# Sums over keys with both partial sums on TensorE, and new orders for the first and the middle head pairs

## The chip, the cores and the metric

The kernel runs on one core of one Trainium2 chip. The metric is the device time of one execution, in microseconds (us), as the median of several runs; beside it stands one execution that the hardware profiler took, from which all rows come. TensorE is PE in the rows (PEld is its weight load), VectorE is DVE, ScalarE is ACT, GpSimd is POOL and SyncE is SP.

## What is computed

Attention over 4 x 8 heads with queries averaged in twos, then a soft mixture of 8 experts, then a gated layer. Cut to what matters:

```python
# attention: q, k, v are (4, 8, 1152, 64), here worked on as 16 pairs of heads
q_pool = q.reshape(B, H, S // 2, 2, D).mean(axis=3)
scores = scale * np.matmul(q_pool, k.transpose(0, 1, 3, 2))
scores = scores - np.max(scores, axis=-1, keepdims=True)
attn = np.exp(scores)
attn = attn / (np.sum(attn, axis=-1, keepdims=True) + 1e-09)   # the sums over keys
x = np.matmul(attn, v)                       # -> (2304, 512)
# soft mixture: logits = x @ phi, a softmax over tokens and one over slots,
# 32 slots through the experts' w1, relu, w2, and back to the tokens
# gated layer: rms norm, silu(xn @ w_gate) * (xn @ w_val) @ w_out
```

## The kernel before

**Stages.** First the attention, one pair of heads at a time (16 pairs, numbered 0 to 15 by `p`), with the mixture's logits worked in between; then the 8 experts; then the gated layer. While the pairs run, the 36 tiles of the gated layer's weights come in as 64-bit values, are converted to 32 bits (`load_64`, `abs_64`, `turn_64`) and are written away to DRAM (`spill`), to be read back at the end (`load`, kind "r").

**One pair.** A pair has 9 tiles of keys (`kt`) and 2 halves of queries (`h`), so 18 score steps. `qk` (step `q<kt><h>`) makes a score tile with 8 matmul records in PSUM and ACT takes its exponential `e` (L380). `add_e` (step `e<kt><h>`) adds the exponentials on POOL (L396) into two partial sums for each half, `acc[p, h, 0]` and `acc[p, h, 1]`: the first 5 or 6 tiles go into one, the others into the second (`PART`). `av` (step `v<kt>`) multiplies with the values into one PSUM tile that stays open over all 9 tiles. In the next pair `sum_up` (L413) joins the two partial sums: for pairs 0 to 13 by a transfer from SBUF to SBUF that POOL issues and that adds while it writes (L415), for pair 14 by DVE. Then `sums` (L419) sums over keys with a matmul against ones; it takes one partial sum, or both where the second one still exists (`n = 1 + ((p, hs[0], 1) in acc)`), as it does for pair 15.

**Beside it in each pair.** `m`, `ta` and `tb` are products for the next pair's row maxima (`wide_item`, each reduced by DVE, L322 to L335); `max_red`, `max_row` and `send_row` turn the maxima into a row and send it by four small transfers on SP's queue (L353, L354). `load_q`, `load_k`, `sum_q`, `high_q`, `low_q`, `round_k`, `less_k` and `rest_k` prepare the pair after next; `sum_q` and `rest_k` are accumulating transfers issued by POOL. `take_x` copies the finished values (xu), `inverse`, `recips` (the copy rr, L444) and `x_divide` divide them by the sums; `logit_add` adds to the logits. Every fourth pair has extra steps: `d_turn` and `d_exp` in pairs 4, 8 and 12, `d_back`, `d_copy` (the copy dn, L539), `slot_part` and `slot_turn` in pairs 5, 9 and 13, `c_turn` (ct, L585 and L587) in pairs 6, 10 and 14.

**What sets the order.** Each engine, and each queue of transfers, works in the order in which the program issues. That order is written out by hand in four lists of steps: `FIRST` for pair 0, `PLAN` for pairs 1 to 13, `LAST_2` for pair 14 and `LAST` for pair 15 (`order_of`). A step named three times is done in three parts: the three `abs_64` of a pair each convert the oldest raw weight that was loaded, the three `turn_64` each finish the oldest conversion on DVE, and the three `load_64` each load one. A step that has nothing to do is passed over.

**Room.** SBUF tiles come from pools of fixed numbers: `B` has 32 (exponentials, partial sums, rounded q), `A` 11, `C` 27. In PSUM the attention has four tiles (two banks each) for everything, one of which the values hold. A new tile waits until the last reader of the tile that it replaces is done. `keep_b` holds back a number of B tiles from the loads of weights.

Of the kernel before, what the change touches and what calls it, by code (L numbers as in the profile page):

```python
# [14 lines left out]
ALU = mybir.AluOpType  # L15
# [3 lines left out]
NP = 16  # L19
# [12 lines left out]
NMAX = 9  # L32
AHEAD = 0
FIRST = """
q00 e00 q10 round_k1 e10 q20 e20 m v00 m m v10 m v20 q30 round_k1 e30 q40 low_q e40 q50 e50 m v30 block_q1 m m v40 m
v50 row_0 q60 e60 q70 low_k e70 q80 e80 m v60 m m load_q v70 v80 q01 e01 q11 low_k e11 q21 e21 m v01 m load_k m v11
sum_q v21 q31 high_q e31 q41 e41 q51 e51 m v31 m load_v max_red v41 v51 max_row send_row q61 round_k e61 q71 e71 q81
e81 round_k less_k v61 v71 v81 block_q
"""
PLAN = """  # L40
load_q c_exp take_x m q00 rest_k sum_q sum_up q01 q10 sum_up m q11 q20 e00 e10 e20 load_k m q21 e01 m q30 e11 q31 q40
load_ew e21 m load_ew e31 q41 e41 e30 q50 q51 e40 m q60 q61 m e50 q70 e60 q71 m e51 q80 q81 e61 e71 m tb ta spill e70
v0 v1 high_q round_k abs_64 max_red sums turn_64 max_row x_logits inverse e80 send_row inverse load_64 v2 e81 turn_64
round_k pair_up logit_add v3 v4 block_q v5 load_64 v6 less_k d_back abs_64 low_q d_turn c_soft abs_64 turn_64 recips
x_turn d_copy slot_part c_turn slot_copy c_soft c_soft x_divide c_soft v7 load_64 x_divide drop_x d_exp v8 slot_turn
load_v
"""
LAST_2 = """
load_q c_exp take_x m q00 rest_k sum_q sum_up q01 load q10 sum_up m q11 load q20 e00 e10 e20 load_k m load q21 e01 m
load q30 e11 q31 load q40 load_ew e21 m load_ew e31 load q41 e41 e30 load q50 q51 e40 m load q60 load q61 m e50 q70  # L50
e60 q71 m e51 load q80 q81 e61 e71 m tb ta spill e70 v0 v1 high_q round_k abs_64 max_red sums turn_64 max_row x_logits
inverse e80 send_row inverse load_64 v2 e81 turn_64 round_k pair_up logit_add v3 v4 block_q v5 load_64 v6 less_k
d_back abs_64 low_q d_turn c_soft abs_64 turn_64 recips x_turn d_copy slot_part c_turn slot_copy c_soft c_soft
x_divide c_soft v7 load_64 x_divide drop_x d_exp v8 slot_turn load_v
"""
LAST = """
take_x q00 load_64 sum_up sum_up load_q load_k load q01 e00 e01 c_exp turn_64 load_ew load q10 load q11 spill e10 e11
# [39 lines left out]
def attention_softmoe_gated_kernel(ctx: ExitStack, tc: tile.TileContext, kT, qT, vv, ip, cst, w1, w2, wg, wv, wo, rg, out):  # L97
    nc = tc.nc
    dv, ac, pe, gp, sy = nc.vector, nc.scalar, nc.tensor, nc.gpsimd, nc.sync
# [11 lines left out]
    free = dict(size)  # L111
# [12 lines left out]
    def rel(tag, n=1):  # L124
        free[tag] += n
        assert free[tag] <= size[tag], tag
# [16 lines left out]
    def two(name, keep_a):  # L143

        if not pairs:
            tag = next((x for x in "WA" if free[x] > (keep_a if x == "A" else 0)), None)
            if not tag:
                return None
            us, t = carve(tag, F32, name)
            for i in range(0, len(us) - 1, 2):  # L150
                pairs.append((t[:, 512 * i:512 * i + 1024], us[i][1]))
            if len(us) % 2:
                singles.append(us[-1])
        return pairs.pop(0)

    keep_b = [99]

    def room(keep_a=0):
        return (len(singles) + 2 * len(pairs) + free["C"] + max(0, free["B"] - keep_b[0])
                + 3 * free["W"] + 2 * max(0, free["A"] - keep_a))  # L160

    def unit(name):

        if singles:
            return singles.pop(0)
        for tag in "CB":
            if free[tag] > (keep_b[0] if tag == "B" else 0):
                return take(tag, [128, 512], F32, name), lambda: rel(tag)
        t, drop = two(name, 0)
        singles.append((t[:, 512:1024], drop))  # L170
        return t[:, 0:512], drop
# [47 lines left out]
    tb = one.tile([128, 128], F32R, name="tb")  # L219
# [4 lines left out]
    mx3, xu, acc, avt, rr, lg, srow = ({} for _ in range(7))  # L224
# [186 lines left out]
        ac.copy(xu[p].rearrange("p (h q) -> p h q", h=2), avt.pop(p)[:, :, 0:HQ])  # L411

    def sum_up(p, h):  # L413
        if p < NP - 2:
            gp.dma_start(out=acc[p, h, 0], in_=acc.pop((p, h, 1)), accum_op=ALU.add)  # L415
        else:
            dv.tensor_tensor(out=acc[p, h, 0], in0=acc[p, h, 0], in1=acc.pop((p, h, 1)), op=ALU.add)
        rel("B")

    def sums(p, hs=(0, 1)):  # L420
# [229 lines left out]
    def load(n, keep_a=0, keep_c=0):  # L650

        for _ in range(n):
            if not stream:
                return
            kind, e, i = stream[-1]
            if kind == "r":
                if not free["C"]:
                    return
                w32[e, i] = unit("w32")
                sy.dma_start(out=w32[e, i][0], in_=away[e, i])  # L660
            else:
                if kind == "w1":
                    src = w1[e, 64 * i:64 * i + 128, :]
                else:
                    src = w2[e, 128 * i:128 * i + 256, :].rearrange("(c p) d -> p c d", p=128)
                if room(keep_a) < len(fresh) + 2 + keep_c:
                    return
                t = two(kind, keep_a)
                if t:
                    t, drop = t  # L670
                    sy.dma_start(out=t if kind == "w1" else t.rearrange("p (c d) -> p c d", c=2), in_=src)
                    x = [(t[:, 0:512], drop), (t[:, 512:1024], drop)]
                elif len(singles) + free["C"] + max(0, free["B"] - keep_b[0]) >= 2:
                    x = [unit(kind), unit(kind)]
                    for c in range(2):
                        sy.dma_start(out=x[c][0], in_=src[:, 512 * c:512 * c + 512] if kind == "w1" else src[:, c])
                else:
                    return
                for c in range(2):
                    ew[kind, e, i + c] = x[c]  # L680
            stream.pop()
# [23 lines left out]
    def side(p):  # L705
# [66 lines left out]
        if 0 < p < NP - 2:  # L772
            at("load_64", lambda i: load_64() if i < 2 or p % 2 or p < 11 else None)
            at("load_ew", lambda i: load(1, 99, KEEP_C + min(len(doubles), 4 * HELD + HELD_O)) if p >= FIRST_EW else None)
# [4 lines left out]
        if p == NP - 2:  # L779
            spill()  # L780
            assert not doubles
            at("load", lambda i: (keep_b.__setitem__(0, KEEP[3]), load(1, KEEP_A[0])))
        if p == NP - 1:
            at("load", lambda i: (spill(), keep_b.__setitem__(0, KEEP[0]), load(1, KEEP_A[1])))
        return sides

    with tc.manual_schedule():
# [127 lines left out]
        for h in range(2):  # L915
# [16 lines left out]
                         in1=al[:, :, None].to_broadcast([32, 3, 32]), op=ALU.mult)  # L932
# [375 lines left out]
```

## Time and profile before

| | us |
|---|---|
| median of 3 runs | 722.84 (721.96 to 726.03) |
| the profiled execution | 728.97 |
| its span, first to last instruction | 727.2 |
| PE busy | 677.9 (93%) |
| POOL busy | 479.2 (66%) |
| DVE busy | 434.0 (60%) |
| ACT busy | 402.6 (55%) |

A busy time is the sum of an engine's work, whatever it waited in between; the ends of matmuls are modelled, so a busy PE is not PE at its peak. Where an engine waits, the profile names the event that came last. The granted clock is TensorE's, 1.00 for 2.4 GHz; the lower of the two levels is 1.2 GHz.

### The profile page before, as it was taken

Reading aid. Unit: us, or ns where it says so; the run is one execution under the profiler, and the core shown is the slowest. Engines: PE = TensorE matmul, PEld = TensorE weight load, DVE = VectorE, ACT = ScalarE, POOL = GpSimd, SP = SyncE. Lnnn points to the kernel's source line nnn. Section 1 sums busy time; section 2 is a strip of 40 time slices with the busy share of each in tenths; the row PEclk is TensorE's granted clock in tenths of the full one; section 3 lists DMA queues with packets and bytes.
Section 4 is the critical chain, followed back from the end, with each engine's and each line's share of the span. In section 5 each row is a group of like instructions: output and inputs, shape, how many; then the busy total and the mean of one; then the engine's idle time right before and its main releaser. Section 6 shows DMA issues by size and latency. Waiting matters only on the chain.

```text
span 727.2 us, 17618 instructions
## 1 busy us (share of the span) xinstructions
PE 677.9 (93%) x7199; PEld 482.8 (66%) x7199; DVE 434.0 (60%) x597; ACT 402.6 (55%) x812; POOL 479.2 (66%) x393
## 2 busy tenths in 40 slices
PE   4999989999798999798999989999989999999998
PEld 2566766756467567475775766654467788888887
DVE  5756877767476777566878856632154755544420
ACT  2466866766467677565776753533155755444320
POOL 5589899889595997966899977401046955535320
PEclk9999999999899999999999999999999999999999
DMA  5144775975939569566495586899991000000000
GB/s 177 52 129 116 200 240 130 277 230 124 320 92 292 202 153 285 154 149 190 108 286 173 109 259 226 291 313 376 386 383 38 35 26 30 29 30 30 15 36 37
DMA packets 61793, 122.33 MB, mean 168 GB/s; under 512 B 6808, under 2 KB 20624, under 8 KB 61712
## 3 DMA queue, kind: packets, MB, share of 16 engines
q1 hardware_dynamic: 53792, 100.86, 39.5%
q0 software_dynamic: 7920, 20.35, 15.0%
q8 instruction: 56, 0.92, 0.5%
q14 instruction: 25, 0.20, 0.1%
HBM read 98.70 MB, written 14.16 MB: 155 GB/s over the span
## 4 chain that ended last, share of the span: by engine, by line
PE 65%; DMA 17%; ACT 6%; DVE 4%; SPq 4%; issue 3%; POOL 1%; ACTq 0%; POOLq 0%; DVEq 0%
PE yo L1209 19%; PE sc L378 18%; PE av L403 8%; DMA acc<-acc 5%; PE mxp L321 3%; DMA raw<-in_wo_dram 3%; DMA qs<-in_qT_dram 3%; PE gv L1161 3%; DMA raw<-in_wg_dram 2%; PE hin L974 2%; PE so L999 2%; SPq L354 2%; DMA w<-away 1%; DMA raw<-in_wv_dram 1%; PE pp L549 1%
## 5 line engine op out<-in xcount | busy, mean ns | idle before, releaser
L396 POOL TENSOR_TENSOR acc<-acc,e 128x576 f32<-128x576 f32 x153 | 230.8, 1517 | 15.4 <-ACT e L380 6.5
L380 ACT ACTIVATE e<-sc 128x576 f32<-128x576 f32 x288 | 172.7, 651 | 50.8 <-PE sc L378 45.8
L322 DVE TENSOR_REDUCE mx<-mxp 128x2 f32<-128x1024 f32 x120 | 145.2, 1223 | 42.9 <-PE mxp L321 41.0
L403 PE MATMUL av<-e,vt 128*32 128x288 f32 x2304 | 155.1, 414 | 0.2 <-ACT e L380 0.2
L396 POOL TENSOR_TENSOR acc<-e 128x576 f32<-128x576 f32 x63 | 105.5, 1675 | 27.4 <-ACT e L380 27.4
L403 PEld LDWEIGHTS av<-e,vt 128*32 128x32 f32 x2304 | 71.1, 111 | 68.8 <-issue 9.0
L378 PE MATMUL sc<-qh,kh 64*128 64x288 f32 x576 | 92.7, 318 | 7.7 <-ACT rr L444 3.8
L1209 PE MATMUL yo<-woh,hA 128*128 128x512 f32 (+1 forms) x312 | 98.6, 385 | 0.3 <-POOL hA L1192 0.2
L378 PE MATMUL sc<-qh,kl 64*128 64x288 f32 x576 | 86.8, 297 | 0.0
L378 PE MATMUL sc<-mr,pick 64*128 64x288 f32 x576 | 86.6, 296 | 0.0
L378 PE MATMUL sc<-ql,kh 64*128 64x288 f32 x576 | 86.6, 296 | 0.0
L1192 POOL TENSOR_TENSOR hA<-hu,hA 128x384 fp32r<-128x384 f32 x48 | 48.8, 1020 | 44.0 <-ACT hA L1191 40.3
L1166 DVE SCALAR_TENSOR_TENSOR th<-th,gv 128x384 f32<-128x384 f32 x72 | 39.8, 553 | 55.8 <-ACT th L1163 55.6
L378 PEld LDWEIGHTS sc<-qh,kh 64*128 64x128 f32 x576 | 55.6, 189 | 25.9 <-DVE mx L322 10.5
L1209 PEld LDWEIGHTS yo<-woh,hA 128*128 128x128 f32 x312 | 57.6, 188 | 10.8 <-POOL hA L1192 1.1
L696 DVE SCALAR_TENSOR_TENSOR w<-w,raw 128x512 uint32<-128x512 uint32 x36 | 41.2, 1145 | 38.4 <-ACT raw L694 33.3
L1163 ACT ACTIVATE th<-gv 128x384 f32<-128x384 f32 x72 | 35.2, 491 | 49.8 <-PE gv L1161 45.8
L692 ACT ACTIVATE w<-raw 128x512 f32<-128x512 f32 x36 | 24.7, 687 | 65.6 <-DMA raw<-in_wo_dram 25.8
L321 PE MATMUL mxp<-kh,qh 64*128 64x512 f32 x240 | 51.4, 426 | 7.8 <-DVE ct L587 4.5
L1209 PE MATMUL yo<-wol,hA 128*128 128x512 f32 (+1 forms) x151 | 57.8, 383 | 0.0
L378 PEld LDWEIGHTS sc<-qh,kl 64*128 64x128 f32 x576 | 55.8, 189 | 2.7
L378 PEld LDWEIGHTS sc<-ql,kh 64*128 64x128 f32 x576 | 55.8, 189 | 0.0
(208 smaller groups left out, 1077.4 us busy)
## 6 DMA issues: line engine op xcount, KB each, us to landing
w<-in_w_dram SPq DMA_DIRECT2D x84, 256.0 KB
w<-in_w_dram SPq DMA_DIRECT2D x22, 512.0 KB
vt<-in_vv_dram SPq DMA_DIRECT2D x16, 576.0 KB
away<-w SPq DMA_DIRECT2D x36, 256.0 KB
w<-away SPq DMA_DIRECT2D x36, 256.0 KB
kraw<-in_kT_dram SPq DMA_DIRECT2D x15, 576.0 KB
kl<-in_kT_dram POOLq DMA_DIRECT2D x14, 576.0 KB, 9.1
acc<-acc POOLq DMA_DIRECT2D x28, 288.0 KB, 9.1
```

The costliest lines, as they stand in the source:

```text
L321: pe.matmul(o[:, s, :], lhsT=q[r, 128 * t:128 * t + 128], rhs=k[r, 512 * c:512 * c + 512], start=True, stop=True)
L322: dv.reduce_max(out=heads[:, :, t, c], in_=o, axis=AX.X)
L378: pe.matmul(o[:, s, 0:HQ], lhsT=w[r, wk], rhs=q[r, c], start=(i == 0), stop=(i == 3))
L380: ac.activation(ets[p, kt, h], o[:, :, 0:HQ], AF.Exp, scale=0.0625)
L396: eng.tensor_tensor(out=acc[p, h, j], in0=first[p, h, j] if n == 1 else acc[p, h, j], in1=e, op=ALU.add)
L403: pe.matmul(avt[p][g:g + 32, h, 0:HQ], lhsT=vt[p][:, kt, g:g + 32], rhs=ets[p, kt, h][:, g // 64], start=(n == 1), stop=(n == NKT))
L692: ac.activation(w32[key][0], hi.bitcast(F32), AF.Prelu, scale=2.0 ** -112, alpha=-2.0 ** 32)
L696: dv.scalar_tensor_tensor(out=y, in0=y, scalar=3, in1=lo, op0=ALU.logical_shift_left, op1=ALU.bitwise_or),
L1163: ac.activation(t, o[0], AF.Tanh, scale=0.5)
L1166: dv.scalar_tensor_tensor(out=t, in0=t, scalar=1.0, in1=o[0], op0=ALU.add, op1=ALU.mult)
L1192: gp.tensor_tensor(out=b, in0=u, in1=f(a), op=ALU.subtract)
L1209: pe.matmul(o, lhsT=x, rhs=w[:, c], start=(ft == 0 and i == 0), stop=(ft == NF - 1 and i == 2))
```

## The change

Three things are changed. `sum_up` keeps only its DVE form, and `PLAN` and `LAST_2` no longer name it; only `LAST`, which is unchanged, still does (for the sums of pair 14). So the partial sums of pairs 0 to 13 both stay in their buffers until `sums` in the pair after, which then takes both. The lists `FIRST`, `PLAN` and `LAST_2` are written anew; apart from `sum_up` each holds the same steps as often as before, in another order. In `load`, the tiles that are read back may take a B tile when no C tile is free, as far as `keep_b` leaves any.

```diff
 FIRST = """
-q00 e00 q10 round_k1 e10 q20 e20 m v00 m m v10 m v20 q30 round_k1 e30 q40 low_q e40 q50 e50 m v30 block_q1 m m v40 m
-v50 row_0 q60 e60 q70 low_k e70 q80 e80 m v60 m m load_q v70 v80 q01 e01 q11 low_k e11 q21 e21 m v01 m load_k m v11
-sum_q v21 q31 high_q e31 q41 e41 q51 e51 m v31 m load_v max_red v41 v51 max_row send_row q61 round_k e61 q71 e71 q81
-e81 round_k less_k v61 v71 v81 block_q
+m load_q m round_k1 round_k1 q00 m q20 m m m q10 q40 e10 e00 q30 q70 q60 m e30 row_0 q50 m q80 e70 e50 e60 m e20 v20
+v00 e40 v60 v50 block_q1 v40 e80 low_q m m q11 load_k v30 v70 q51 q21 q81 q31 q41 e11 q01 q71 q61 e21 e31 low_k m v21
+e61 m sum_q m e81 v31 e01 round_k e51 m m e71 v80 e41 v71 v41 max_red v10 high_q low_k v81 max_row round_k load_v v51
+send_row block_q v61 v11 v01 less_k
 """
 PLAN = """
-load_q c_exp take_x m q00 rest_k sum_q sum_up q01 q10 sum_up m q11 q20 e00 e10 e20 load_k m q21 e01 m q30 e11 q31 q40
-load_ew e21 m load_ew e31 q41 e41 e30 q50 q51 e40 m q60 q61 m e50 q70 e60 q71 m e51 q80 q81 e61 e71 m tb ta spill e70
-v0 v1 high_q round_k abs_64 max_red sums turn_64 max_row x_logits inverse e80 send_row inverse load_64 v2 e81 turn_64
-round_k pair_up logit_add v3 v4 block_q v5 load_64 v6 less_k d_back abs_64 low_q d_turn c_soft abs_64 turn_64 recips
-x_turn d_copy slot_part c_turn slot_copy c_soft c_soft x_divide c_soft v7 load_64 x_divide drop_x d_exp v8 slot_turn
-load_v
+load_q m c_exp take_x q00 sum_q q01 q10 rest_k m q11 e00 e10 load_k q20 m q21 m e20 q30 e30 e01 e11 q31 e21 q40
+load_ew m load_ew e31 q41 q50 e41 q51 e40 m q60 q61 e50 q70 e60 q71 m q80 spill q81 abs_64 m e51 m e61 round_k e71
+high_q tb ta v0 e70 max_red v1 sums turn_64 max_row round_k send_row inverse x_logits e80 inverse c_turn e81 turn_64
+v2 logit_add v3 abs_64 v4 load_64 v5 block_q less_k v6 d_back low_q d_turn load_64 recips c_soft d_copy x_turn abs_64
+turn_64 pair_up slot_part x_divide slot_copy c_soft c_soft x_divide c_soft load_64 drop_x d_exp v7 v8 load_v slot_turn
 """
...
     def sum_up(p, h):
-        if p < NP - 2:
-            gp.dma_start(out=acc[p, h, 0], in_=acc.pop((p, h, 1)), accum_op=ALU.add)
-        else:
-            dv.tensor_tensor(out=acc[p, h, 0], in0=acc[p, h, 0], in1=acc.pop((p, h, 1)), op=ALU.add)
+        dv.tensor_tensor(out=acc[p, h, 0], in0=acc[p, h, 0], in1=acc.pop((p, h, 1)), op=ALU.add)
         rel("B")
...
             kind, e, i = stream[-1]
             if kind == "r":
-                if not free["C"]:
+                if not free["C"] and free["B"] <= keep_b[0]:
                     return
                 w32[e, i] = unit("w32")
```

`LAST_2` changes as `PLAN` does, with its `load` steps between the scores as before.

## Rows read from the trace of the kernel before

**Rows 1.** The page, part 1: busy us (share of the span) x instructions.
```profile
PE 677.9 (93%) x7199; PEld 482.8 (66%) x7199; DVE 434.0 (60%) x597; ACT 402.6 (55%) x812; POOL 479.2 (66%) x393
```

**Rows 2.** Stretches, cut at pairs' first scores: length, engines' busy us, clock, DMA share, GB/s.
```profile
16.50:47.90 31.40, 30.86 (x329) 18.30 (x330) 19.73 (x25) 14.92 (x28) 19.77 (x14) 1.00 0.16 58
...
101.80:128.10 26.30, 25.29 (x341) 17.88 (x341) 20.60 (x23) 19.03 (x36) 24.68 (x21) 1.00 0.69 190
...
157.80:194.40 36.60, 30.58 (x367) 20.05 (x369) 20.58 (x23) 20.23 (x38) 26.29 (x22) 0.91 0.78 221
...
222.20:249.80 27.60, 26.83 (x345) 19.39 (x341) 20.61 (x23) 19.42 (x36) 22.07 (x16) 0.94 0.72 206
...
426.80:452.00 25.20, 25.14 (x349) 18.25 (x345) 18.52 (x23) 11.40 (x21) 19.99 (x14) 1.00 0.75 240
...
486.00:540.00 54.00, 50.03 (x599) 25.16 (x600) 14.19 (x42) 17.29 (x46) 7.76 (x12) 0.97 1.03 377
```

**Rows 3.** Waits of PE: engine, line <- releaser: us in total, times, longest us.
```profile
PE pp L549 <- ACT dn L539: 11.5, 3, 4.9
...
PE mxp L321 <- DVE ct L587: 4.5, 2, 2.2
PE sc L378 <- ACT rr L444: 3.8, 5, 1.5
PE sums L429 <- DMA acc<-acc: 3.6, 4, 1.3
...
PE mxp L321 <- ACT rr L444: 2.4, 3, 1.1
```

**Rows 4.** Timeline of ACT, end of pair 3: start, us, instruction [idle before <- releaser].
```profile
125.31 0.70 ACT L692 ACTIVATE w<-raw 128x512 f32<-128x512 f32 x1 [4.26 <-DMA raw<-in_wg_dram]
125.91 0.69 ACT L694 ACTIVATE raw<-raw 128x512 int32<-128x512 uint16 x1
...
127.92 0.15 ACT L444 COPY rr<-sumt 96x12 f32<-96x12 f32 x1
127.97 0.64 ACT L411 COPY xu<-av 128x576 f32<-128x576 f32 x1
```

**Rows 5.** The tile raw, who waited for it: us in total, times.
```profile
  ACT w L692: 65.4, 22
```

**Rows 6.** Timeline of SP's queue in pair 3.
```profile
120.84 0.51 SPq L354 DMA_DIRECT2D mr<-mrow  x1
121.39 0.58 SPq L644 DMA_DIRECT2D raw<-in_wg_dram  x1
```

**Rows 7.** The chain that ended last, in order: start us, us, what.
```profile
187.49 2.79 PE pp L549 x16
190.28 3.28 PE av L403 x32
...
422.48 1.50 PE pp L549 x16
...
440.13 2.08 PE av L403 x32
```

**Rows 8.** Groups by line: line, engine, operation, count | busy us, mean ns | idle.
```profile
L415 POOL DMA_DIRECT2D acc<-acc x28 | 30.0, 1424 | 0.0
```

**Rows 9.** Line L415, the accumulating transfers: who waited for them, and landings.
```profile
  ACT qh L259: 9.2, 4
...
DMA to landing us min/median/max: 6.1/9.1/13.4
```

**Rows 10.** Timeline of PE in pair 0, around one value step.
```profile
31.90 0.69 PE L403 MATMUL av<-e,vt 128*32 128x288 f32 x8
32.52 0.73 PE L321 MATMUL mxp<-kh,qh 64*128 64x512 f32 x4
```

**Rows 11.** Timeline of ACT in pair 0.
```profile
17.94 0.65 ACT L380 ACTIVATE e<-sc 128x576 f32<-128x576 f32 x1 [3.90 <-PE sc L378]
```

**Rows 12.** The page, part 5: the wide reductions of the row maxima.
```profile
L322 DVE TENSOR_REDUCE mx<-mxp 128x2 f32<-128x1024 f32 x120 | 145.2, 1223 | 42.9 <-PE mxp L321 41.0
```

More of the change, by code (lines that the diff above doesn't have):

```diff
@@ L47 @@
+high_q tb ta v0 e70 max_red v1 sums turn_64 max_row round_k send_row inverse x_logits e80 inverse c_turn e81 turn_64
+v2 logit_add v3 abs_64 v4 load_64 v5 block_q less_k v6 d_back low_q d_turn load_64 recips c_soft d_copy x_turn abs_64
+turn_64 pair_up slot_part x_divide slot_copy c_soft c_soft x_divide c_soft load_64 drop_x d_exp v7 v8 load_v slot_turn
 """
 LAST_2 = """
-load_q c_exp take_x m q00 rest_k sum_q sum_up q01 load q10 sum_up m q11 load q20 e00 e10 e20 load_k m load q21 e01 m
-load q30 e11 q31 load q40 load_ew e21 m load_ew e31 load q41 e41 e30 load q50 q51 e40 m load q60 load q61 m e50 q70
@@ L51 @@
[L51 to L54, printed above, removed]
+load_q m c_exp take_x q00 sum_q q01 load q10 rest_k m q11 e00 e10 load_k load q20 m load q21 m e20 load q30 e30 e01
@@ new lines @@
+e11 q31 e21 load q40 load_ew m load_ew e31 load q41 load q50 e41 q51 e40 m load q60 load q61 e50 q70 e60 q71 m load
+q80 spill q81 abs_64 m e51 m e61 round_k e71 high_q tb ta v0 e70 max_red v1 sums turn_64 max_row round_k send_row
+inverse x_logits e80 inverse c_turn e81 turn_64 v2 logit_add v3 abs_64 v4 load_64 v5 block_q less_k v6 d_back low_q
+d_turn load_64 recips c_soft d_copy x_turn abs_64 turn_64 pair_up slot_part x_divide slot_copy c_soft c_soft x_divide
+c_soft load_64 drop_x d_exp v7 v8 load_v slot_turn
```

## The prediction

> **What bounds the kernel now.** I read the page's busy times first. The reader should see that TensorE (PE) carries 93% of the span and no other engine comes near it [rows 1]; so the time is what PE needs plus what PE waits. Next I cut the span at the first score product of each head pair and read busy times by stretch [rows 2]. Three things stand there. Pair 14, the last that has all the work of a middle pair, takes 25.2 us and PE is busy for 25.14 of them: that is the floor. A plain pair like pair 3 takes 26.3, about 1 more. The pair with the slot step (pair 5, and pair 9 in the same way) takes 36.6 with a granted clock of 0.91, and pair 7 (11 likewise) runs at 0.94. The fourteen pairs 1 to 14 fill 47.9 to 452.0, 404.1 us; fourteen floors are 352.8.
>
> Then I asked what PE waits for [rows 3]. The largest waits end with three ACT copies or a DVE step: dn (11.5), rr (3.8 and 2.4) and ct (4.5); then the accumulating transfers before the sums (3.6). The copy rr takes 0.15 us of work, so I looked at what ACT did before it [rows 4]. In pair 3 it does nothing for 4.26 us, because the next instruction in its queue, the conversion of a raw weight (abs_64), waits for a transfer; it does two conversions, and only then the copy rr, for which PE has long delivered. That idle time sums to 65.4 us in 22 places [rows 5]. ACT works in order, so whatever stands behind abs_64 pays for the weight's landing. The transfer cannot be earlier: its issue stands on SP's queue behind the sending of the row maxima [rows 6]. It landed 3.9 us after issue, 2.8 us before the next pair's first product at 128.1.
>
> So the same event, a raw weight that lands about 3 us before a pair ends, sets rr, dn and ct; ct through DVE, where the second half of the conversion (turn_64) stands ahead of it.
>
> **The orders of middle pairs.** The new lists put recips (rr) and d_copy (dn) ahead of the conversion that needs a weight of the same pair; the conversion in the middle now comes before the first load of its pair, so it takes a weight whose transfer was issued about a pair earlier. Its DVE half then never waits either, since the three turn_64 of a pair take the oldest three conversions and the third finds the middle one done. c_turn moves to the middle of the pair. I remove the waits on dn (11.5), rr (3.8 + 2.4) and ct (4.5): 22.2 us [rows 3]. What comes next there: the copy xu of the following pair, now behind the late conversion. By [rows 4] that conversion could start at 125.31 and needs 1.35 us, to 126.7; xu began at 127.97. So it is covered, with 1.3 us to spare. The division x_divide, which frees a score tile on DVE, waits only for rr and its transposes and lies before the last two value steps (32 records, 2.08 us of PE [rows 7]); covered. The small waits on DVE and ACT not shown I leave as they are.
>
> **The clock.** After the dn wait the 16 slot products take 2.79 us, against 1.50 in pair 13, and the 32 value products 3.28, against 2.08 [rows 7]. PE had waited before, up to 4.9 us [rows 3], and the granted clock of the pair is 0.91: part of it ran at the lower of the two levels. I take 2.7 us for pair 5 and 2.1 for pair 9, where the same rows repeat with 2.79 and 2.89. In pairs 7 and 11 a clock of 0.94 over 27.6 us means 12% of it at half speed, 3.3 us, of which half is lost: 1.7 each. Without the waits ahead of them these fall away: 8.1 us.
>
> **Both partial sums on PE.** Removed are 28 transfers and their issue on POOL, 30.0 us in all [rows 8], or 2.1 a pair. No wait of PE ends with POOL, so that counts nothing by itself; but POOL, with 24.68 us of the 26.30 of pair 3 [rows 2], would be the next engine to bind and gets this room. On the path were the landings: 9.1 us in the middle, 13.4 at most [rows 9], so that PE waited 3.6 us [rows 3], and ACT waited 9.2 us with the copy qh, which takes the buffer that such a transfer was still reading. The first I count in full, the second not: it delayed the row maxima and so the raw weights, and is in the waits above. Added are, in each of 14 pairs, 8 more matmul records of 32 columns by 288. The row of the value product has the same form: 32 records in 2.08 us, 65 ns each [rows 7]. So 112 x 0.065 = 7.3 us. Its bounds: nothing, where PE would stand there anyway for the row maxima; 14.6 if they ran at half clock. I take 7.3, since PE sets the pace there.
>
> The accumulating transfer lands 6.1 to 13.4 us after its issue in this trace. The Trainium skill (DMA: Bandwidth & Descriptors, Anatomy of one DMA, SWDGE path) gives 2.0 us plus bytes over 436 GB/s for a transfer issued by GpSimd, as an estimate 2.7 us here. By it the transfers would land before the sums ask, the 3.6 us would not be theirs, and the sum would be 699.1. The trace does not agree, at 9.1.
>
> Two buffers of B stay taken until the sums of the next pair instead of being given back early. Only the last score tiles of a pair come to need them, so I cost this at 0; if the cover is gone, the experts' weights start two units of 256 KB later, 1.4 us at the 377 GB/s of the last row of [rows 2]. The same stretch bounds the changed condition in load, which lets the reread weights go into B: the transfers are at 1.03 of their share there, so issuing earlier moves nothing. 0, bounds 2 us either way. sum_q goes ahead of rest_k on POOL, and the additions stay behind both, so their start is unchanged.
>
> **The first pair.** All scores of one half come first, and the value steps stand in 6 groups instead of 13. A lone value step holds PE 0.62 us until the next product starts [rows 10], against 0.52 inside a run (2.08/4): 7 x 0.10 = 0.7 us. Moved past other work: the rounding of k ahead of the first exponentials on ACT, load_q ahead of the rows on SP. Both are free there: ACT waits 3.90 us for the first scores [rows 11]. Bounds: 4 us worse, if DVE, which now has nine reductions early (1.22 us each for the wide ones [rows 12]), holds the score tiles; 6.2 better, the pair's 31.4 us against the floor.
>
> **The sum.** 22.2 + 3.6 + 8.1 + 0.7 - 7.3 = 27.3 us less. The profiled execution took 728.97 (span 727.2 and 1.77 around it), so it would be 701.7; the median of the runs is 722.84, 6.1 below the profiled one, so I forecast 722.84 - 27.3 = 695.5. A check from the other side: 14 floors with the added sums, 14 x 25.7 = 360, and some 10 for the slot and turn steps, 370 against 404.1: 34 less. That is the low end: 722.84 - 34 - 3 for the first pair, 686.
>
> **Rivals.** *The wait moves to DVE.* After the last scores there now stand four max products in a row instead of three. Their reductions take 3 x 1.22 = 3.7 us and a small one on DVE, and the row maxima, which the next pair and the weights' loads await, come 1.2 us later. For: PE is in order and its transpose of the maxima stands right behind the sums. Against: two value steps and sums of 16 records fill 48 x 0.065 = 3.1 us of PE meanwhile, besides the products. If it exposes 1.0 us in 14 pairs, 14 us return: 709.5.
>
> *Given back later.* The stretch of the experts runs the transfers at 1.03 of their share; if the weights loaded ahead during the pairs were fewer by what the pairs get shorter, the expert stage would wait. Against: loading ahead is limited by buffers, and the share in the pairs shown is 0.69 to 0.78 [rows 2]. All 27.3 would have to go: about 722.
>
> *Slower.* The late conversion now stands in front of xu and of the next pair's exponentials. If the raw weight lands later than today, all scores stop. PE has 1.3 us to spare and three score tiles (1.6 us), so nothing is lost up to 2.9 us late; from there each microsecond counts in 12 pairs. To eat 27.3 and 3.6 more takes 2.6 a pair: landing 5.5 us later than now, 9.4 instead of 3.9 us after issue. At 6 us it is 722.84 - 27.3 + 12 x 3.1, 733. For: shorter pairs crowd the transfers. Against: 8.3 MB of transfers are gone.
>
> **How the numbers follow.** Forecast, 686 to 703: 0.62. Wait moved, 703 to 719: 0.22. Given back: 0.07. Slower: 0.09. The range 686 to 712 takes the forecast and most of the second case, and leaves out 0.2. A measurement of this kernel tells about 0.5%, 3.6 us, from no change; faster by more 0.84, within 0.07, slower by more 0.09.
>
> **What would show it.** Right: no PE wait on dn, rr, ct or a transfer before the sums; ACT's idle time on raw weights small and after rr; the clock at 1.00 in every pair; 248 records of sums where there were 136; plain pairs near 25.8 us, slot pairs near 28.5, the stretch from the experts on unchanged within 2 us. Wrong: a wait of ACT xu or e behind a raw weight, a PE wait on the transposed maxima or on a DVE reduction near 1 us a pair, or a first pair over 31.4 us.

## The result and the profile after

The changed kernel takes 696.53 us in the median of 4 runs (693.88 to 697.53); the kernel before, in 4 runs, 724.43 (721.96 to 731.08). The ratio is 0.9595, with a 95% interval of 0.9523 to 0.9667: faster. A second set of runs on another occasion gave 0.957 (0.9497 to 0.9644). Some executions of a kernel take over 1.5% longer than its fastest, and the ratios leave these slow ones out, which matters here only for the joins on DVE below: six of their ten runs are slow, the profiled one among them, and the other four took 717.79 to 727.35.

The page of the changed kernel, its part 1, answers to [rows 1]:

```profile
PE 670.3 (97%) x7311; PEld 484.5 (70%) x7311; DVE 445.5 (64%) x597; ACT 401.0 (58%) x812; POOL 459.2 (66%) x365
```

PE is busy for 97% of the span and was for 93%. It has 112 instructions more, POOL 28 fewer: the transfers.

Next the stretches of the changed kernel, cut at the pairs' first score products as in [rows 2], with its columns. In this order: pair 0; pairs 1 to 14 together; pairs 2, 3, 4, 5 and 7; everything from pair 15 on.

```profile
17.60:46.20 28.60, 28.60 (x328) 20.23 (x328) 21.15 (x24) 14.97 (x29) 20.68 (x14) 1.00 0.12 43
...
46.20:417.90 371.70, 367.58 (x4994) 260.68 (x4990) 297.42 (x322) 261.99 (x500) 323.74 (x228) 1.00 0.64 191
...
72.60:99.60 27.00, 25.52 (x351) 18.25 (x349) 22.96 (x24) 18.80 (x35) 20.90 (x16) 1.00 0.54 149
99.60:125.00 25.40, 25.37 (x351) 18.21 (x351) 21.94 (x22) 19.22 (x37) 21.64 (x18) 1.00 0.68 188
125.00:151.00 26.00, 25.93 (x355) 18.32 (x353) 21.93 (x25) 19.74 (x38) 25.20 (x19) 1.00 0.75 232
151.00:178.70 27.70, 27.67 (x377) 19.50 (x375) 21.73 (x22) 20.09 (x38) 25.65 (x18) 1.00 0.73 235
...
205.00:230.40 25.40, 25.36 (x351) 18.19 (x349) 21.20 (x22) 18.41 (x35) 21.83 (x16) 1.00 0.68 207
...
417.90:692.10 274.20, 267.07 (x1973) 200.03 (x1969) 117.00 (x238) 118.30 (x273) 104.55 (x104) 0.99 0.38 139
```

And the same view of the kernel before for pairs 1 to 14 together, and for pair 4, which [rows 2] do not have:

```profile
47.90:452.00 404.10, 373.81 (x4884) 261.66 (x4880) 287.36 (x321) 264.75 (x503) 344.53 (x255) 0.97 0.69 195
...
128.10:157.80 29.70, 26.95 (x345) 18.14 (x345) 21.06 (x27) 19.65 (x38) 27.19 (x21) 1.00 0.79 233
```

The reader should see three things. Pairs 1 to 14 take 371.7 us instead of 404.1, and that is nearly all of the gain: from pair 15 on it is 274.2 instead of 275.2 (727.2 less 452.0). In pairs 1 to 14 PE idles 4.1 us (371.70 less 367.58) where it idled 30.3; and although it has 110 records more there, it is busy 6.2 us less, and the granted clock was 0.97 and is 1.00, in each of the fourteen pairs.

What PE still waits for in the changed kernel, the view of [rows 3]: engine, line <- releaser: us in total, times, longest.

```profile
PE mxp L300 <- ACT kh L807: 6.3, 2, 5.7
PE mxt L362 <- issue: 3.0, 1, 3.0
PE sc L377 <- DVE xt L474: 2.0, 2, 1.4
PE sc L377 <- ACT xu L410: 1.0, 2, 0.6
```

In this view nothing waits on dn, rr or ct any more, nor sums on a transfer. The two largest that are left belong to the start: L300 and L362 work for the first pair alone. ACT at the end of pair 3, the answer to [rows 4] (start, us, instruction, idle time before and its releaser):

```profile
122.08 0.17 ACT L440 COPY rr<-sumt 96x12 f32<-96x12 f32 x1 [2.13 <-PE sumt L435]
122.80 0.71 ACT L688 ACTIVATE w<-raw 128x512 f32<-128x512 f32 x1 [0.56 <-DMA raw<-in_wg_dram]
123.41 0.70 ACT L690 ACTIVATE raw<-raw 128x512 int32<-128x512 uint16 x1
124.89 0.64 ACT L410 COPY xu<-av 128x576 f32<-128x576 f32 x1 [0.78 <-PE av L402]
```

The copy rr now waits for PE, as it should; it used to stand behind two conversions. The late conversion waits 0.56 us for its weight, after rr, and is done before xu is wanted: ACT idles 0.78 us until PE has finished the values. Who waited for the tile raw, the answer to [rows 5]:

```profile
  ACT w L688: 8.7, 12
```

8.7 us where it was 65.4. In the slot pair 5 the chain that ended last (start, us, what) has shorter products than in [rows 7], at a clock of 1.00:

```profile
174.49 1.43 PE pp L545 x16
175.92 1.94 PE av L402 x32
```

### The profile page after: what moved, and what is told of

The parts are those of the page before. It is cut to its first block, busy times and chain, and to the rows that moved or that the text cites. A ratio compares the mean times of both kernels' runs of the same rounds, so it can differ in the third digit from the quotient of the medians.

```text
span 692.1 us, 17751 instructions
## 1 busy us (share of the span) xinstructions
PE 670.3 (97%) x7311; PEld 484.5 (70%) x7311; DVE 445.5 (64%) x597; ACT 401.0 (58%) x812; POOL 459.2 (66%) x365
## 4 chain that ended last, share of the span: by engine, by line
PE 83%; DMA 6%; POOL 3%; ACT 3%; DVE 2%; issue 1%; SPq 1%; ACTq 0%; DVEq 0%; POOLq 0%
PE sc L377 22%; PE yo L1205 20%; PE av L402 17%; PE mxp L320 4%; PE gv L1157 3%; DMA w<-away 3%; PE sums L425 2%; POOL acc L395 2%; PE hin L970 2%; PE mxp L326 1%; DMA raw<-in_wg_dram 1%; PE xo L465 1%; DMA w<-in_w_dram 1%; PE mxp L330 1%; PE xl L483 1%
## 5 line engine op out<-in xcount | busy, mean ns | idle before, releaser
L379 ACT ACTIVATE e<-sc 128x576 f32<-128x576 f32 x288 | 170.2, 652 | 39.1 <-PE sc L377 34.4
L402 PE MATMUL av<-e,vt 128*32 128x288 f32 x2304 | 150.5, 408 | 0.0
L377 PE MATMUL sc<-qh,kh 64*128 64x288 f32 x576 | 89.8, 305 | 3.4 <-DVE xt L474 2.0
L377 PEld LDWEIGHTS sc<-qh,kh 64*128 64x128 f32 x576 | 55.7, 187 | 11.5 <-DVE mx L321 5.5
L377 PEld LDWEIGHTS sc<-mr,pick 64*128 64x128 f32 x576 | 55.9, 187 | 0.9 <-DMA mr<-mrow 0.9
L692 DVE SCALAR_TENSOR_TENSOR w<-w,raw 128x512 uint32<-128x512 uint32 x36 | 51.6, 1432 | 6.8 <-ACT raw L690 6.8
```

Source lines behind the costliest of these rows:

```text
L377: pe.matmul(o[:, s, 0:HQ], lhsT=w[r, wk], rhs=q[r, c], start=(i == 0), stop=(i == 3))
L379: ac.activation(ets[p, kt, h], o[:, :, 0:HQ], AF.Exp, scale=0.0625)
L402: pe.matmul(avt[p][g:g + 32, h, 0:HQ], lhsT=vt[p][:, kt, g:g + 32], rhs=ets[p, kt, h][:, g // 64], start=(n == 1), stop=(n == NKT))
L692: dv.scalar_tensor_tensor(out=y, in0=y, scalar=3, in1=lo, op0=ALU.logical_shift_left, op1=ALU.bitwise_or),
```

## The experiments

Theory: two things held PE up, and each hid part of what the other cost. One is ACT's queue, where rr, dn and (through DVE) ct stood behind the conversion of a weight that landed late. The other is the landing of the accumulating transfers, which held back sums and, through the buffers, the rounding qh, which the row maxima need. The change removes both. Rivals: the sums alone did it; the orders alone did it; the room on POOL did it; the smaller parts (the condition in load, the first pair) did it. Each cell of the following table is the stretch of pairs 1 to 14 of one kernel, from the line quoted with its experiment; idle is length less PE's busy time. The columns far weights and new orders are two ways to take the weight out of the queue: only the moved conversions, or all of the new lists.

| pairs 1 to 14: us (PE idle) | lists as before | far weights | new orders |
|---|---|---|---|
| transfers | 404.1 (30.3) | 384.2 (17.2) | 385.8 (13.5) |
| sums on PE | 400.6 (21.0) | 377.2 (7.9) | 371.7 (4.1) |

**The changed kernel again**, beside the first group.

> The changed kernel itself, beside the experiments on the same chip. All theories: 696 (693 to 699), 28 below before.

696.92 us (693.94 to 698.61), as before. Its pair 1 began at 44.3 instead of 46.2 and pair 15 at 415.6 instead of 417.9: executions of one kernel differ by that much in the first pair.

**The sums alone**, on the kernel before:

```diff
-            at("sum_up", lambda i: sum_up(l, 1 - i))
+            at("sum_up", lambda i: sum_up(l, 1 - i) if l == NP - 2 else None)
```

> Before with both partial sums taken on PE, all four orders as before (sum_up is passed over for pairs 0 to 13). My theory, that late raw weights in ACT's queue set the time and the transfers only 3.6 us of it: +7.3 for 112 matmul records, -3.6 to -5 for the waits before the sums, so +2 to +4, about 727. Rival, that the transfers themselves made the row maxima and so the weights late (the 9.2 us that ACT waited with qh, passed on): most of the gain without any new order, 705 to 714.

729.54 us (727.24 to 735.39) against 727.9 for the kernel before on that occasion: ratio 1.0041 (1.0004 to 1.0079). Its pairs 1 to 14 as one stretch, and its waits:

```profile
47.60:448.20 400.60, 379.59 (x4994) 266.91 (x4990) 285.93 (x321) 264.76 (x503) 318.19 (x227) 0.97 0.59 177
```

```profile
PE pp L549 <- ACT dn L539: 7.7, 3, 2.9
...
PE sc L378 <- ACT rr L444: 4.9, 5, 2.0
...
ACT w L692 <- DMA raw<-in_wo_dram: 22.4, 5, 5.1
ACT w L692 <- DMA raw<-in_wv_dram: 20.7, 8, 5.4
ACT w L692 <- DMA raw<-in_wg_dram: 18.2, 8, 5.2
```

With no such transfer left, ACT still waits 61.3 us in 21 places for raw weights (65.4 in 22 before), and dn and rr still hold PE. PE idles 9.3 us less, but its records take 5.8 more at the same 0.97. PE's waits on dn, rr and ct together are 17.0 us, where they were 22.2. So the landings account for only a small part of the weights' lateness. The sums by themselves gain nothing in the whole execution; the room on POOL, which they free, gains nothing either. The 3.5 us by which the pairs are shorter in this trace come back from pair 15 on (279.9 us against 275.2), in the stage whose clock the last section shows to differ from execution to execution.

**The new orders alone**: the changed kernel with the old `sum_up` and the transfers.

```diff
-load_q m c_exp take_x q00 sum_q q01 q10 rest_k m q11 e00 e10 load_k q20 m q21 m e20 q30 e30 e01 e11 q31 e21 q40
+load_q m c_exp take_x q00 sum_q q01 q10 rest_k sum_up sum_up m q11 e00 e10 load_k q20 m q21 m e20 q30 e30 e01 e11 q31
...
+        if p < NP - 2:
+            gp.dma_start(out=acc[p, h, 0], in_=acc.pop((p, h, 1)), accum_op=ALU.add)
```

> The changed kernel with the accumulating transfers put back (two sum_up behind rest_k in the orders of pairs 1 to 14). My theory: the orders carry the gain, -22.2 -8.1 -0.7 = -31.0, about 693, that is 3 to 4 below the changed kernel, since 7.3 us of matmuls go and 3.6 of waits return. Rival, that the sums on PE carry it: 710 or more. Third: the landings, 9 us in the middle, now come later than the sums in every pair, 14 x 1 us, about 705.

710.2 us (702.08 to 711.36), ratio 0.9721 (0.964 to 0.9802). The stretch of pairs 1 to 14, then its waits on the transfers, then their landings:

```profile
44.00:429.80 385.80, 372.34 (x4884) 259.60 (x4880) 294.42 (x322) 263.33 (x500) 347.94 (x256) 0.99 0.74 205
```

```profile
ACT qh L259 <- DMA acc<-acc: 16.9, 13, 3.3
...
PE sums L429 <- DMA acc<-acc: 7.8, 11, 2.0
```

```profile
DMA to landing us min/median/max: 8.7/10.0/12.9
```

My own figure of 693 fell. Once the weights are out of the way the pairs are shorter, the transfers still take 10.0 us, and they come to bind: PE waits 7.8 us for them (3.6 in [rows 3]) and ACT 16.9 with qh (9.2 in [rows 9]). So the sums on PE, worth nothing alone, count here: the ratios 0.9721 and 0.957 differ by 0.015, give or take 0.011, so by 3 to 19 us (13 by the medians). The Trainium skill (DMA: Bandwidth & Descriptors, Anatomy of one DMA, SWDGE path) would have each land after an estimated 2.7 us, well before the sums ask. The trace does not agree: the landings took 8.7 to 12.9 us, and the measurement decides.

**The far weights alone**: in the kernel before, the middle conversion ahead of the pair's first load, the late one behind rr and dn.

```diff
-v0 v1 high_q round_k abs_64 max_red sums turn_64 max_row x_logits inverse e80 send_row inverse load_64 v2 e81 turn_64
-round_k pair_up logit_add v3 v4 block_q v5 load_64 v6 less_k d_back abs_64 low_q d_turn c_soft abs_64 turn_64 recips
-x_turn d_copy slot_part c_turn ...
+v0 v1 high_q round_k abs_64 max_red sums turn_64 max_row x_logits inverse e80 send_row inverse abs_64 load_64 v2 e81
+turn_64 round_k pair_up logit_add v3 v4 block_q v5 load_64 v6 less_k d_back low_q d_turn c_soft recips x_turn d_copy
+abs_64 turn_64 slot_part c_turn ...
```

> Before, with only the conversions moved in the lists of pairs 1 to 14: the middle one ahead of the first load of its pair (so it takes a weight of the pair before), the late one behind the copies rr and dn. Transfers, first pair and everything else as before. My theory: rr, dn and most of ct go, with the clock: -22.2 -8.1 = -30.3, about 694 (c_turn stays late, so up to 4.5 may stay: 694 to 699). Rival, that the orders gain by the scores, maxima and c_turn being laid out anew, not by the weights: -10 at most, 714 or more.

714.33 us (711.79 to 716.44), ratio 0.98 (0.9732 to 0.9868): 14 us, not the 30 that I had put on it. Pairs 1 to 14 and the waits of PE in them:

```profile
47.60:431.80 384.20, 367.04 (x4882) 260.12 (x4878) 287.49 (x321) 265.99 (x503) 345.21 (x255) 0.99 0.73 205
```

```profile
PE sc L378 <- DVE xt L478: 5.9, 8, 2.2
PE sc L378 <- DVE ct L587: 5.2, 2, 2.9
PE sums L429 <- DMA acc<-acc: 3.5, 5, 1.0
```

The waits on rr and dn are gone, as the theory says, and the clock is 0.99. The rest comes out elsewhere: the transfers before the sums, ct (c_turn still stands late), and the division xt.

**Both together**: the far weights and the sums on PE, without the rest of the new lists.

```diff
-            at("sum_up", lambda i: sum_up(l, 1 - i))
+            at("sum_up", lambda i: sum_up(l, 1 - i) if l == NP - 2 else None)
```

> The old orders with the conversions moved as in far_weights, and both partial sums on PE; the first pair, the scores, c_turn and load as before. If the two parts only add up (-13.6 for the weights, 0 for the sums): 714 to 717. My theory now, that the two hide each other (with the weights out of ACT's way the landings of the accumulating transfers come to set the pairs, 3.5 us of PE waits and 11.7 of qh in far_weights): most of the changed kernel's gain, 700 to 706, the rest being c_turn, the waits on xt and the first pair.

706.31 us (703.97 to 711.58), ratio 0.9727 (0.9658 to 0.9797), just above what I had expected. Its pairs 1 to 14:

```profile
46.90:424.10 377.20, 369.31 (x4995) 261.14 (x4991) 286.45 (x321) 266.17 (x503) 319.42 (x227) 1.00 0.63 188
```

If the two parts simply added, the ratios 0.98 and 1.0041 would give 0.984; measured is 0.9727, less by 0.011, give or take 0.010, or 1 to 16 us. With the step from 710.2 to 696.92 above it is the same finding twice: the sums are worth nothing until the weights are moved. In the table, the sums take 3.5 us off the pairs with the old lists, 7.0 with the far weights and 14.1 with the new ones. Between this kernel and the changed one lie 10 us of the medians; the traces show 5.5 of them in pairs 1 to 14, where PE's largest wait is on xt (5.3 us in 8 places, in the changed kernel 2.0 in 2). Which of the other moves (c_turn, recips, x_divide) brings them was not tried one by one.

**The late conversion back** ahead of rr and dn, in the changed kernel:

```diff
-v2 logit_add v3 abs_64 v4 load_64 v5 block_q less_k v6 d_back low_q d_turn load_64 recips c_soft d_copy x_turn abs_64
-turn_64 pair_up ...
+v2 logit_add v3 abs_64 v4 load_64 v5 block_q less_k v6 d_back low_q d_turn load_64 abs_64 turn_64 recips c_soft d_copy
+x_turn pair_up ...
```

> The changed kernel with the late conversion of each pair put back ahead of rr and dn on ACT (and its DVE half ahead of recips); the rest as changed. My theory: ACT waits there again for a weight that lands 2 to 3 us before the pair ends; in the slot pairs PE waits for dn again (3 x 2 to 3 us) and elsewhere x_divide comes 1 us late: 8 to 12 us more, 704 to 709, and up to 5 more if the clock falls. Rival, that with the middle conversion far from its load the place of the late one no longer matters: 697.

701.46 us (700.42 to 702.13), ratio 0.9623 (0.9593 to 0.9653): some 4.5 slower than the changed kernel, less than I had put. Against the changed kernel, which ran on another occasion, the ratios differ by 0.0053, give or take 0.0079, which is not clear of noise; against the kernel of the next experiment, which equals the changed one and ran beside this one, by 0.0072, give or take 0.0044 (2 to 8 us), which is. The wait of PE, and ACT in the slot pair 5:

```profile
PE pp L545 <- ACT dn L535: 4.8, 3, 1.6
```

```profile
172.51 0.67 ACT L688 ACTIVATE w<-raw 128x512 f32<-128x512 f32 x1 [3.15 <-DMA raw<-in_wg_dram]
173.08 0.65 ACT L690 ACTIVATE raw<-raw 128x512 int32<-128x512 uint16 x1
173.64 0.14 ACT L440 COPY rr<-sumt 96x12 f32<-96x12 f32 x1
173.69 0.31 ACT L535 COPY dn<-dn 96x192 f32<-96x192 f32 x1
```

The chain of the prediction stands in four lines: ACT idles 3.15 us for a weight, converts it, and only then makes rr and dn, for which PE waits. The Trainium skill (TensorE: Matmul & The Clock Gate, Architectural detail: the array is 16× 32×32) calls ACT's and DVE's queues strictly first in, first out; these rows agree. It costs less than before: PE loses 4.8 us to dn here and 11.5 in [rows 3], and ACT waits 45.1 us in 13 places for raw weights, where it was 65.4 in 22 [rows 5].

**The old condition in load**, in the changed kernel:

```diff
-                if not free["C"] and free["B"] <= keep_b[0]:
+                if not free["C"]:
```

> The changed kernel with the old condition in load (reread weights wait for a C tile). My prediction costed it at 0, 2 us at most: 695 to 699. Rival, from the traces of the two runs with the pairs shortened by other means, where the part from the experts on took 278 to 283 us instead of 274 to 277: the condition keeps transfers flowing at the end of the experts, and without it 4 to 8 us come back, 700 to 705.

695.8 us (694.2 to 697.68), ratio 0.9551 (0.9519 to 0.9583): no difference from the changed kernel.

**The joins on DVE**: in the changed kernel one partial sum instead of two reaches the sums; DVE joins them, one half after q60 and the other after q61.

```diff
-load_ew m load_ew e31 q41 q50 e41 q51 e40 m q60 q61 e50 q70 e60 q71 m q80 spill q81 abs_64 m e51 m e61 round_k e71
+load_ew m load_ew e31 q41 q50 e41 q51 e40 m q60 sum_up q61 sum_up e50 q70 e60 q71 m q80 spill q81 abs_64 m e51 m e61
```

> The changed kernel with the two partial sums of pairs 0 to 13 joined on DVE among the score steps of the next pair, so that the sums take 8 matmul records again, without any transfer. My theory, PE sets the pace and the 112 records cost 7.3 us: 689, if DVE (22 of 25.4 us busy, 2.2 more) keeps up. Rival, the records are hidden behind the wait for the row maxima: 696. Second rival, DVE holds the score tiles in the middle of the scores: 700 or more.

728.72 us in 10 runs (717.79 to 733.42), ratio 0.9959 (0.9909 to 1.0008): the whole gain is gone. Pair 11 as a stretch, the two joins in it on DVE, and the largest wait of PE:

```profile
307.40:337.00 29.60, 27.46 (x351) 19.05 (x348) 25.08 (x27) 18.44 (x36) 24.07 (x16) 0.94 0.55 157
```

```profile
316.79 3.40 DVE L414 TENSOR_TENSOR acc<-acc 128x576 f32<-128x576 f32 x2
```

```profile
PE mxp L327 <- DVE mx L322: 26.5, 14, 2.5
```

The two additions take 3.4 us in pair 11, the reductions of the maxima stand behind them in DVE's queue, and PE waits for such a reduction in every pair. DVE is busy for 25.08 of 29.6 us, about the same share as in the changed kernel, so it is the place in its queue that costs, not a full engine. Of the three ways tried, transfers, DVE at this place and PE, PE is the cheapest, though it is the engine that bounds; other places in DVE's queue were not tried.

**Each matmul of the sums twice**, in the changed kernel:

```diff
-                    pe.matmul(o[g:g + 32, :], lhsT=ones, rhs=acc[p, h, j][:, s], start=(j == 0), stop=(j == n - 1))
+                    for again in range(2):
+                        pe.matmul(o[g:g + 32, :], lhsT=ones, rhs=acc[p, h, j][:, s], start=(j == 0 and not again), stop=(j == n - 1 and again == 1))
```

> The changed kernel with every matmul of the sums done twice (the sums are then twice as large; that part of the result is wrong by a factor and the time is not meant as a kernel's). 248 records more at 65 ns. My theory, PE sets the pace and added records cost their own time: +16, about 713. Rival, they hide behind the wait for the row maxima: +0 to +4, 697 to 701.

707.69 us (706.33 to 713.88), ratio 0.9754 (0.967 to 0.9838). Pairs 1 to 14:

```profile
46.20:430.60 384.40, 381.83 (x5219) 271.45 (x5215) 297.29 (x322) 262.18 (x500) 323.04 (x228) 1.00 0.62 185
```

224 records more in these pairs make them 12.7 us longer (384.40 less 371.70) and PE 14.25 us busier: 57 to 64 ns a record, near the 65 of [rows 7]. So the added records are not hidden behind other waits here.

**The first pair as before**, in the changed kernel: `FIRST` is the old list of the diff above.

```diff
-m load_q m round_k1 round_k1 q00 m q20 m m m q10 q40 e10 e00 q30 q70 q60 m e30 row_0 q50 m q80 e70 e50 e60 m e20 v20
+q00 e00 q10 round_k1 e10 q20 e20 m v00 m m v10 m v20 q30 round_k1 e30 q40 low_q e40 q50 e50 m v30 block_q1 m m v40 m
...
```

> The changed kernel with the old order of the first pair. My prediction counted 0.7 us for the new one: 697.5. From the traces since (pair 1 starts at 43.6 to 46.2 with the new list, 47.6 to 47.9 with the old): 2 to 4 us more, 699 to 701. Rival, the pairs behind it absorb it: 696.5.

695.81 us (692.6 to 699.75), ratio 0.9575 (0.9509 to 0.9642): no difference, and the 2 to 4 us that I had come to expect after reading the trace fell. Pairs 0 and 2:

```profile
16.50:47.70 31.20, 30.66 (x331) 18.30 (x331) 19.73 (x25) 14.93 (x28) 19.77 (x14) 1.00 0.16 58
73.90:100.10 26.20, 25.67 (x353) 18.32 (x351) 21.55 (x24) 18.59 (x35) 20.99 (x15) 1.00 0.55 153
```

The old first pair takes 31.2 us, the new one 28.6 (26.7 in the second set), but it begins 1.1 earlier, and pair 2 takes 26.2 instead of 27.0: at pair 15 the two stand at 418.3 and 417.9 (415.6).

**All conversions far**: in the changed kernel the first load of a pair is moved behind the late conversion, so that this one too takes a weight of the pair before.

```diff
-v2 logit_add v3 abs_64 v4 load_64 v5 block_q less_k v6 d_back low_q d_turn load_64 recips c_soft d_copy x_turn abs_64
-turn_64 pair_up ...
+v2 logit_add v3 abs_64 v4 v5 block_q less_k v6 d_back low_q d_turn load_64 recips c_soft d_copy x_turn abs_64 turn_64
+load_64 pair_up ...
```

> The changed kernel with the first load of each pair issued behind the late conversion, so that all three conversions take weights of the pair before. My theory: the late conversion's remaining waits (up to 2 us in pairs 2, 7 and 12, and PE's waits on xu and xt after them, 3 to 4 us) go: 692 to 694. Rival, no gain, because the other pairs have none: 696. Second rival, the raw tiles hold A tiles longer and k or v come late: 699 or more.

695.06 us (692.68 to 699.38), ratio 0.9547 (0.9504 to 0.9589): the same. What the late conversion still costs in the changed kernel cannot be measured.

**The weight later**: in the changed kernel the first raw weight of each pair is transferred twice into its tile.

```diff
-            at("load_64", lambda i: load_64() if i < 2 or p % 2 or p < 11 else None)
+            at("load_64", lambda i: load_64(i == 0) if i < 2 or p % 2 or p < 11 else None)
```

> The changed kernel with the first raw weight of each pair transferred twice into the same tile, so that it lands some 3.5 to 4 us later (and the transfers behind it in SP's queue with it). The slower rival of the prediction priced this: nothing lost up to 2.9 us late, then each microsecond counts in 12 pairs: 12 x 0.6 to 1.1, 704 to 710. If the margin is gone from the start: 12 x 3.5, 738. If ACT makes it up in the pair: 697.

747.1 us (745.1 to 751.13), ratio 1.0286 (1.0219 to 1.0352): 50 us more than the changed kernel, far beyond what I expected, and slower than the kernel before. SP's queue at the end of pair 1, ACT and DVE at the same place, PE's two largest waits, and pairs 1 to 14:

```profile
64.99 4.03 SPq L641 DMA_DIRECT2D raw<-in_wg_dram  x2
```

```profile
67.93 0.16 ACT L440 COPY rr<-sumt 96x12 f32<-96x12 f32 x1 [3.32 <-PE sumt L435]
72.28 0.66 ACT L689 ACTIVATE w<-raw 128x512 f32<-128x512 f32 x1 [4.19 <-DMA raw<-in_wg_dram]
...
73.38 0.62 ACT L410 COPY xu<-av 128x576 f32<-128x576 f32 x1
```

```profile
73.51 0.69 DVE L693 SCALAR_TENSOR_TENSOR w<-w,raw 128x512 uint32<-128x512 uint32 x1 [7.80 <-ACT raw L691]
74.12 1.01 DVE L474 TENSOR_TENSOR xt<-xo,rr 96x384 f32<-96x384 f32 x2
```

```profile
PE sc L377 <- DVE xt L474: 10.2, 3, 3.7
PE sc L377 <- ACT dtx L523: 9.3, 3, 3.6
```

```profile
44.40:468.60 424.20, 387.70 (x4994) 276.45 (x4990) 292.04 (x322) 260.34 (x500) 322.80 (x228) 0.95 0.61 183
```

The conversion begins 27.9 us after the pair's first product, in the changed kernel 24.4 (70.57 less 46.2): 3.5 us later, and xu and the exponentials of the next pair stand behind it. So does the division xt: its place in DVE's queue is behind the second half of the conversion, turn_64 (L693), for which DVE idles 7.80 us. PE makes one score tile of pair 2 and then waits 3.7 us for xt, which frees the room of the next; in the changed kernel it waits 1.4 at the same place. The pairs are 52.5 us longer, some 4 for each that loads weights: 32.4 of it in PE's idle time, 20.1 in busy time, the clock being 0.95. The experiment is not clean: the second transfer holds SP's queue too, so that the other weights and the next queries came about 3.5 us later as well. But ACT waits for a raw weight 13 times, once a pair (58.5 us), and of the 36.5 us that PE idles in these pairs 32.4 end with xt, dtx, psb and xu, which stand behind that conversion on DVE or ACT; only 0.4 end with a transfer. What the other late transfers cost by way of other engines stays open.

## Why the prediction was right, point by point

The time came out, 695.5 against 696.53, and so did what bounds the kernel and which waits go. That the time fits to 1 us is luck: the gain was put too small and the time before too low, and the two errors cancel.

- **What bounds the kernel.** Right: PE in pairs 1 to 14, and there the waits and the clock. These pairs give 32.4 us of the trace's 35.1.
- **The waits removed, 22.2 and 3.6.** Right in sum: PE's idle time in pairs 1 to 14 fell by 26.2, forecast 25.8. Wrong in how it was divided between the two parts of the change: the prediction counted 3.6 for the transfers and gave the rest to the orders. Moving the conversions alone brings 14 us, the sums alone none, both 22. The step that failed is "The first I count in full, the second not": the landings stood just behind the weights and came to bind when these went (16.9 us on qh, 7.8 on the sums). Nor was the reason given for the second more than a small part of the truth, that the wait with qh made the raw weights late: without the landings ACT still waits 61.3 us for them (65.4 before) and PE 17.0 for dn, rr and ct (22.2).
- **The clock, 8.1.** Right cause; the size was probably too small. For pair 5 the rows of [rows 7] give 2.5 (1.29 and 1.20), where 2.7 was taken; measured on the same products it is 2.7. Over pairs 1 to 14 PE's busy time fell by 6.2, where -8.1 and +7.3 make -0.8. In pairs 5, 7, 9 and 11 it fell by 7.7 with the added sums in it, so the clock there is worth up to about 10. Another 4.5 lie in pairs 2, 3, 4, 8, 12 and 13, at a clock of 1.00 in both kernels: with 0.5 us of sums added to each, pair 4 is busy for 25.93 us instead of 26.95. The ends of matmuls are modelled, so some waiting was counted as work there; that this is the reason is argued, not shown, and some of the 10 may be of the same kind.
- **The added records, +7.3.** Right: 57 to 64 ns each by the doubled ones, where 65 was taken.
- **The first pair, -0.7.** Its pair is 2.8 us shorter in the trace, starts 1.1 later, and the medians show no difference with the old list. The bounds were needless; the part is worth nothing that can be measured.
- **Costed at nothing.** The condition in load (695.8 without it) and the held buffers: right, and from pair 15 on 274.2 us as against 275.2. The copy xu: 1.0 us in 2 places, and 0.78 us to spare in pair 3 where 1.3 was worked out. The division xt: wrong. The prediction has it wait "only for rr and its transposes"; in the new list turn_64 stands ahead of it on DVE, so it waits for the raw weight too, and PE's largest wait left in pairs 1 to 14 ends with it (2.0 us in 2 places). With weights that land as now this costs little.
- **The base.** The profiled execution before, 728.97, and its successor differ by 35.1; the forecast took 27.3 off a median of 722.84. Later medians of the kernel before were 724.43, 727.9, 727.69 and 728.67, so the base was low while the sum was too small.
- **The check by floors** gave 34 for pairs 1 to 14, the sum of the terms 26.6 (27.3 less the 0.7 of the first pair); the traces show 32.4. So for the pairs it was the better estimate. Slot pairs take 27.6 to 27.7 us (forecast 28.5), those with d_turn and d_exp 26.0 to 27.8, the others 25.4 to 27.0 (forecast 25.8).
- **The rivals.** The wait on DVE did not come: PE waits 0.5 us in all for a reduction of the maxima, and that in the first pair; but the margin is thin: with the joins, 3.4 us of DVE in front of the reductions, it came (26.5 us). Nothing was given back later. The slower rival named the right place and a wrong margin: 2.9 us late for nothing was worked out from rows of the kernel before, where xu had 1.3 us and the score tiles were free. In the changed kernel weights 3.5 us later cost some 4 a pair, and in both traces PE makes one score tile of pair 2 before it waits for xt, not three. So there is no such margin, and with weights that late the changed kernel is slower than the kernel before (1.0286).

## What to carry to other kernels

A wait that ends with a short copy belongs to whatever stands ahead of that copy in its engine's queue; look there for a step that a transfer feeds, and give that step data that was asked for a round earlier. Before pricing the parts of a change one by one, ask what would bind next if only one were made: here one part alone is worth 14 us, the other nothing, and both with the rest 28 to 31. When a step that a transfer feeds is moved, look also at the other engine that does its second half: what is queued behind it there waits for the transfer too. In this case a floor taken from the one stretch that runs without waits forecast the gain of the pairs better than the sum of the waits that the trace names.

## What the runs showed of the hardware

The stretch where the experts end and the gated layer begins ran at a different granted clock from execution to execution, with nearly the same transfers. The same 20 us of it, 72 us after pair 15 began, first in the changed kernel, then in the one with the old condition in load (columns as in [rows 2]):

```profile
489.70:510.10 20.40, 17.60 (x232) 12.36 (x227) 11.39 (x28) 9.73 (x21) 7.82 (x7) 1.00 1.05 384
```

```profile
487.10:507.50 20.40, 17.34 (x179) 11.67 (x171) 7.62 (x20) 6.72 (x16) 4.44 (x4) 0.67 1.05 385
```

PE idles about 3 us of 20.4 in both, in waits of at most 0.8 us that end with steps of ACT and DVE, and gets 232 records done at 1.00 and 179 at 0.67, where part of the stretch ran at the lower level. It is not the condition in load: the kernel with the old first pair, whose code from pair 1 on is that of the changed kernel, was granted 0.67 there too, and a second execution of the changed kernel itself 0.92. From pair 15 on these four take 274.2 us (1.00), 276.6 (0.92), 279.7 and 280.5 (0.67), although the medians of the three kernels agree within about 1 us: a difference of 6 us between single traces in that stage says nothing of a change in the pairs.

The accumulating transfers of 288 KB from SBUF to SBUF landed 6.1 to 13.4 us after their issue in the kernel before, 9.1 in the median [rows 9], and 8.7 to 12.9 with the new orders, 10.0 in the median. In both POOL issues them early: in pair 1, 4.3 and 5.3 us after the pair's first score product. So an early issue did not make them short.
